# Local values loaded without the overlap of their blocks, the leading rows copied on the chip (strided sparse attention with a bilinear feed-forward layer)

## The chip, the cores and the metric

The kernel runs on one core of one Trainium2 chip. The metric is the device time of one execution in microseconds (us), the median of several runs. The five engines of the core are named as in the profile: PE (TensorE), DVE (VectorE), ACT (ScalarE), POOL (GpSimd) and SP (SyncE). Each works through its own list of instructions in order, and waits for others through semaphores.

## The reference, cut to what matters

Eight batches of eight heads, 576 positions, 64 values per head. Heads 0 to 3 attend to the last 32 positions only ("local"), heads 4 to 7 to positions at multiples of 32 ("strided"). The result, laid out as 4608 tokens of 512 values, goes through `(x @ w_a) * (x @ w_b) @ w_out`.

```python
scores = scale * np.matmul(q, k.transpose(0, 1, 3, 2))
rel = pos[:, None] - pos[None, :]
mask_local = (rel >= 0) & (rel < 32)
mask_strided = (rel >= 0) & (pos[None, :] % 32 == pos[:, None] % 32)
# heads 0..3 take mask_local, heads 4..7 mask_strided; masked scores become -1e9
attn = exp(scores - max) / (sum(exp(scores - max)) + 1e-09)
x = np.matmul(attn, v)            # then to 4608 x 512
out = ((x @ w_a) * (x @ w_b)) @ w_out
```

A local query sees only itself and 31 keys before it. So the kernel cuts the 576 positions of a head into six blocks of 96 queries, and needs for each block 128 keys and values: the 32 rows before the block and its own 96. Successive blocks overlap by 32 rows.

## The kernel before

The local values of a batch stand in a tile `vl_buf[b % 2]`, 128 partitions by 24 blocks (4 heads x 6), each block 64 values, a column of ones for the sums, and space up to 128 columns. Partition 0 to 31 (`PAD = 32`) of a block hold the rows before it, partitions 32 to 127 its own. The transfer reads float32 and writes bfloat16:

```python
def load_vl(b, blocks=(0, HL * 6)):
    t = vl_buf[b % 2]
    f, e = blocks
    if (b, f) == (0, 0):
        f = 1                       # block 0 of batch 0 has no rows before it
    src = bass.AP(tensor=v.tensor, offset=(b * H * S + LW * f - PAD) * D,
                  ap=[[D, 128], [LW * D, e - f], [1, D]])
    nc.gpsimd.dma_start(out=t[:, f:e, 0:D], in_=src)
```

All large loads are issued by POOL (`nc.gpsimd.dma_start`). They use eight semaphores in turn: a load may be issued when the load eight places before it has landed. The end of the list that matters here, with the semaphore number that each takes, is

```text
... wo_sb (2)  wo_sb (3)  wo_sb (4)  wo_sb (5)  vl of batch 1 (6)  [memset vs]
    kl (7) kl (0) kl (1) kl (2)  ql (3) ql (4) ql (5) ql (6)   natk (7) (0) (1) (2)   natq (3) (4) (5) (6)
```

where `kl`, `ql`, `natk`, `natq` are keys and queries of batch 2. The fourth `ql` so waits until the `vl` of batch 1 has landed.

Batch 0 runs in a hand-made order, whose letters are: `T` transposes of q and k, `S` scores (`p` product on PE, `x` exponential on ACT, `m` mask on DVE), `V` the product with the values (`p` on PE, `r` reciprocal and `n` scaling on DVE), `X` the transpose of the result, `F` the first matmuls of the feed-forward layer, `*n` n filler matmuls on PE, `G` the parts of a mask. An ending number is the unit: 0 to 3 are local, 4 to 7 strided. Units 0 and 1 use value blocks 0 to 11, units 2 and 3 blocks 12 to 23.

```python
ORDER = """
    C0 Tk0p *4 Tq0p Tk0e Tq0e *5 Tk1p S1p M Tq1p S1x Tk1e *4 G0 Tq1e S0p S1m G1 C1 Tq2p S0x Tk2p Tq2e S3p Tk2e G2 S3x *3
    V1p S0m *2 S2p V1r S3m V0p S2x Tk3p V0r Tk3e *1 S4p S2m Tq3p S4x V1n Tq3e *4 V0n S5p S5x X0p X0e *2 V2p V2r V3p V2n
    S6p V4p ...
```

Batches 1 to 7 are interleaved with the feed-forward layer of earlier tokens. Batch 1's local values are first used by `V0` in the middle of the first output matmul block; the table says `12.5: "V0 X2"`:

```python
for i in range(G):                  # G = 3 blocks
    for j in range(2):              # 2 heads
        vt = vl_buf[b % 2][:, (2 * c + j) * 6 + 3 * half + i, 0:D + 1]
        ...
        nc.tensor.matmul(of[:, j, i, :w], lhsT=pt, rhs=vt, start=True, stop=True)
```

In the beginning the rows of block 0 of batch 0 come by a transfer of their own (`raw[2]`) and `C1` casts them into place:

```python
nc.sync.dma_start(out=raw[2][PAD:, :D], in_=v[0, 0, 0:LW, :])
...
elif nm == "C1":
    for p in (slice(PAD, 64), slice(64, 128)):
        nc.vector.tensor_copy(vl_buf[0][p, 0, 0:D], raw[2][p, :D])
```

After batch 0, POOL is given this list at its first place (`do(0, ...)`): fill `vl_buf[0]` with ones, weights, `wo_sb`, `load_vl(1)`, fill `vs_buf[0]`, and then `load_qk(2, ...)`.

Of the kernel before, what the change touches and what calls it, by code (L numbers as in the profile page):

```python
# [7 lines left out]
F32 = mybir.dt.float32  # L8
# [6 lines left out]
FIRST_D = 2  # L15
# [6 lines left out]
LW = 96  # L22
PAD = 32
# [7 lines left out]
def kernel(  # L31
# [10 lines left out]
    nc = tc.nc  # L42
    B, H, S, D = q.shape
# [38 lines left out]
    vl_buf = [const.tile([128, HL * 6, VW], BF16, name=f"vl{i}") for i in range(2)]  # L82
# [15 lines left out]
    def consts(i):  # L98
        if i == 0:
            for p in p_buf:  # L100
                nc.vector.memset(p[:, :, W:], 0.0)
        nc.vector.memset(kT_buf[i][0][:, :, 0:PAD], 0.0)
        nc.vector.memset(kT_buf[i][1], 0.0)
        nc.vector.memset(vl_buf[i][:, :, D:D + 1], 1.0)
        nc.vector.memset(vs_buf[i][:, :, :, D:D + 1], 1.0)
        if i == 0:
            nc.vector.memset(vl_buf[0][:PAD, 0, 0:D], 0.0)

    def fill_v(t):
        nc.gpsimd.memset(t[:, :, :, D:] if len(t.shape) == 4 else t[:, :, D:], 1.0)  # L110
# [21 lines left out]
    def mask_local2():  # L132
        nc.vector.tensor_copy(mask_l, msl.unsqueeze(1).to_broadcast([128, 4, LW]))

        nc.vector.memset(mask_l[:PAD, 0], 0)

    def mask_group(part):

        if part == 0:
            cur["mp"] = psum4["tp"].tile([128, S // 2], F32, tag="tp", name="tp")[:NP, :NP]  # L140
            ef = e4.rearrange("p i r -> p (i r)")
            nc.tensor.matmul(cur["mp"], lhsT=ef, rhs=ef, start=True, stop=True)
        elif part == 1:
            nc.vector.tensor_scalar_mul(mss, cur["mp"], -1.0)

            select(mss, ALU.is_ge, 0, [[1, NP]], -1)
        else:

            nc.vector.tensor_scalar(nmask, mss, 1.0, -8e9, op0=ALU.add, op1=ALU.mult)


    def spin(n):
        for _ in range(n):
            nc.tensor.matmul(cur["misc"][:, :224], lhsT=nc.const_aps.tensor(1.0, [128, 128], BF16),  # L154
                             rhs=nc.const_aps.tensor(1.0, [128, 224], BF16), start=True, stop=True)
# [30 lines left out]
    def load_qk(b, strided, heads=range(HL), names="kq"):  # L186
        for nm in names:
            src = {"k": k, "q": q}[nm]
            if b < FIRST_D:
                n, R, h0 = (NP, RS, HL) if strided else (96, RL, 0)  # L190
                w0 = {"k6": 0, "q6": 1536, "k8": 3072, "q8": 5120}[f"{nm}{R}"]
                if b not in shared:
                    shared[b] = nat.tile([128, FG * 5 * SW], BF16, tag="shared", name="shared")
                t = nats[b, nm, strided] = shared[b][:n, w0:w0 + HL * R * D].rearrange("p (h r d) -> p h r d", r=R, d=D)
                hs = slice(heads[0], heads[-1] + 1)
                nc.gpsimd.dma_start(out=t[:, hs], in_=src[b, h0:h0 + HL].rearrange("h (p r) d -> p h r d", r=R)[:, hs])
            elif strided:

                t = nat_s[nm]
                n = 32 if b == FIRST_D else YS  # L200
                for h in heads:
                    nc.gpsimd.dma_start(
                        out=t[32 * h:32 * h + n],
                        in_=bass.AP(tensor=src.tensor, offset=(b * H + HL + h) * S * D,
                                    ap=[[RS * D, n], [YS * RS * D, 3], [1, RS * D]]))
            else:
                if 0 in heads:
                    nats[b, nm, strided] = nat.tile([128, NY, D], BF16, tag=f"{nm}l", name=f"{nm}l")
                t = nats[b, nm, strided]
                for h in heads:  # L210
                    nc.gpsimd.dma_start(out=t[32 * h:32 * h + 32],  # L211
                                        in_=src[b, h].rearrange("(i y) d -> y i d", y=32))
            nats[b, nm, strided] = t

    def load_vl(b, blocks=(0, HL * 6)):

        t = vl_buf[b % 2]
        f, e = blocks
        if (b, f) == (0, 0):
            f = 1  # L220
        src = bass.AP(tensor=v.tensor, offset=(b * H * S + LW * f - PAD) * D,
                      ap=[[D, 128], [LW * D, e - f], [1, D]])
        nc.gpsimd.dma_start(out=t[:, f:e, 0:D], in_=src)

    def load_vs(b, heads=range(HL)):
        if b < FIRST_D:
# [271 lines left out]
    def step_X(b, c):  # L498
# [6 lines left out]
            "Xp": lambda c: X_p(0, c), "Xe": lambda c: X_e(0, c)}  # L505

    ORDER = """
        C0 Tk0p *4 Tq0p Tk0e Tq0e *5 Tk1p S1p M Tq1p S1x Tk1e *4 G0 Tq1e S0p S1m G1 C1 Tq2p S0x Tk2p Tq2e S3p Tk2e G2 S3x *3
        V1p S0m *2 S2p V1r S3m V0p S2x Tk3p V0r Tk3e *1 S4p S2m Tq3p S4x V1n Tq3e *4 V0n S5p S5x X0p X0e *2 V2p V2r V3p V2n
        S6p V4p V3r V3n V4r V4n S6x X1p V5p V5r S7p X1e V5n V6p S7x X2p V6r V7p V6n X2e Z F0a V7r V7n F0b X3p F1a X3e F0c  # L510
        F1b F1c""".split()

# [229 lines left out]
    with tc.manual_schedule(engines={ENG.PE, ENG.SP, ENG.Pool, ENG.DVE, ENG.Activation}):  # L742
# [6 lines left out]
        nc.vector.memset(ident, 1.0)  # L749

        raw = fsb.tile([128, FD, TTOK], BF16, tag="pf", name="raw", bufs=1)
        raw = [raw[:, 3 * i:3 * i + 3].rearrange("p a b -> p (a b)").bitcast(F32) for i in range(3)]
        for x, src in ((raw[0], k), (raw[1], q)):
            nc.sync.dma_start(out=x[:96].rearrange("p (h r d) -> p h r d", h=2, d=D),
                              in_=src[0, 0:2].rearrange("h (p r) d -> p h r d", r=RL))
        nc.sync.dma_start(out=raw[2][PAD:, :D], in_=v[0, 0, 0:LW, :])
        load_qk(0, False, (2, 3))
        load_qk(0, True, (0, 1), "k")
        select(ident, ALU.is_equal, 0, [[1, 128]], -1)
# [12 lines left out]
        for nm in ORDER:  # L772
            if nm[0] == "*":
                spin(int(nm[1:]))
            elif nm == "C0":
                for x, cp, n in ((raw[0], nc.vector.tensor_copy, "k"), (raw[1], nc.scalar.copy, "q")):
                    cp(nats[0, n, False][:, 0:2].rearrange("p h r d -> p (h r d)"), x[:96])
            elif nm == "C1":
                for p in (slice(PAD, 64), slice(64, 128)):
                    nc.vector.tensor_copy(vl_buf[0][p, 0, 0:D], raw[2][p, :D])  # L780
            elif nm == "M":
                mask_local2()
            elif nm[0] == "G":
                mask_group(int(nm[1]))
                if nm == "G1":
                    load_vs(0)
                    for c in range(2):
                        load_w(c)
                    load_w(2)
                    load_qk(1, True)  # L790
                    load_vs(1)
                    load_w(3)
                    load_qk(1, False)
            elif nm == "Z":
                zero_qz(1, nc.scalar, ((0, 0),))
            elif nm[0] == "F":
                f = int(nm[1])
                if nm[2] == "a":
                    if f == 0:
                        ab = pst.tile([128, 2, 512], F32, tag="st", name="ab")  # L800
                        first[f] = [ab[:, 0], ab[:, 1]]
                    else:
                        first[f] = [psum4[x].tile([128, 512], F32, tag=x, name="ab") for x in ("misc", "o")]
                ab_mm(0, f, first[f], {"a": (0, 1), "b": (2,), "c": (3,)}[nm[2]])
            else:
                PART[nm[:-2] + nm[-1]](int(nm[-2]))
# [16 lines left out]
        def do(i, fn, *args):  # L823
            at.setdefault(i, []).append(lambda: fn(*args))
# [8 lines left out]
        for b in range(FIRST_D, B):  # L833
            g0 = 16 * (b - 2)
            if b == FIRST_D:
                do(0, load_qk, b, False)
                do(1, load_qk, b, True)
                do(16, load_vl, b)
                for h in range(HL):
                    do(18 + h, load_vs, b, (h,))  # L840
            else:
                for h in range(HL):
                    do(g0 + h - (0 if b == FIRST_D + 1 else 2), load_qk, b, False, (h,))
                    do(g0 + h + (6 if b == FIRST_D + 1 else 2), load_qk, b, True, (h,))
                    do(g0 + h + 10, load_vs, b, (h,))
                do(g0 + (10 if b == FIRST_D + 1 else 7), load_vl, b)
            gs = {2: (13, 13, 14, 14, 15, 16, 17, 17, 18, 18), 3: (8, 9, 10, 11, 12, 13, 14, 15, 16, 17)}.get(b) or (
                3, 5, 7, 9, 12, 13, 14, 15, 16, 17)
            for (z, nm, part), g in zip(((0, "k", 0), (0, "k", 1), (0, "q", 0), (0, "q", 1), (1, "k", 0), (1, "k", 1),
                                         (1, "k", 2), (1, "q", 0), (1, "q", 1), (1, "q", 2)), gs):  # L850
                do(g0 + g, step_D, b, z, nm, part)
# [62 lines left out]
```

## Time and profile before

| quantity | value |
|---|---|
| time, median of 3 runs | 332.12 us (331.99 to 332.24) |
| span of the profiled execution | 330.0 us |
| PE busy | 322.2 us (98%) |
| DVE, ACT, POOL busy | 263.8, 202.0, 177.5 us |
| packets of the queue that POOL fills (q0) | 87760, 19.58 MB |
| issues of `vl`: 7 of 384.0 KB, one of 192.0 KB, one of 176.0 KB | 7.2, 5.8, 5.3 us to landing |
| granted clock | 1.000 |

The table is read from the top of the page (busy time), its third part (queues) and its sixth (issues). KB there are bytes written, in bfloat16. A busy PE says that matmuls were in flight, not that each was useful: the filler matmuls count as busy too.

### The profile page before, as it was taken

The page shows a single profiled execution, that of the slowest core. Times are in us where ns is not written, and L with a number is a line of the kernel's source. Part 1 is how long each engine was busy: PE and PEld are TensorE (multiplying, and loading weights), DVE is VectorE, ACT ScalarE, POOL GpSimd, SP SyncE. Part 2 cuts the span into 40 slices and gives each one's busy share as a digit, 9 for nine tenths or more (in the row PEclk, how much of TensorE's full clock was granted, in tenths as well). Part 3 has the DMA queues.
Part 4 walks back from the last instruction along what each step waited for, and adds up shares of the span by engine and source line. Part 5 has one row for each costly group of instructions (what it writes and reads, how often), then busy time and mean ns, then how long its engine had stood idle before and what let it go on. Part 6 is the DMA issues. An engine that isn't in the chain of part 4 may idle for free.

```text
span 330.0 us, 7697 instructions
## 1 busy us (share of the span) xinstructions
PE 322.2 (98%) x2819; PEld 206.4 (63%) x2851; DVE 263.8 (80%) x500; ACT 202.0 (61%) x328; POOL 177.5 (54%) x296
## 2 busy tenths in 40 slices
PE   8999999999999999999999999999999999999995
PEld 6754555455555578556999995559555854584474
DVE  5767586779867999999999999999878944657662
ACT  4763946458777865887677766776777543313321
POOL 8945746299967655775578556845302131132021
PEclk9999999999999999999999999999999999999999
DMA  9999999599999698989988978998024022004004
GB/s 156 145 197 189 202 188 190 135 186 108 126 215 125 117 89 74 84 177 154 91 75 153 186 84 74 133 213 92 22 65 125 0 66 65 0 2 127 3 0 127
DMA packets 100661, 37.60 MB, mean 114 GB/s; under 512 B 77456, under 2 KB 97808, under 8 KB 100624
## 3 DMA queue, kind: packets, MB, share of 16 engines
q0 software_dynamic: 87760, 19.58, 65.3%
q1 hardware_dynamic: 12576, 17.34, 18.1%
q8 instruction: 22, 0.36, 0.4%
q10 hardware_dynamic: 288, 0.20, 0.2%
q14 instruction: 15, 0.12, 0.1%
HBM read 39.71 MB, written 9.44 MB: 149 GB/s over the span
## 4 chain that ended last, share of the span: by engine, by line
PE 83%; DMA 12%; POOL 2%; issue 1%; DVE 1%; ACT 0%; POOLq 0%; DVEq 0%
PE mm L546 50%; PE mm L650 17%; DMA vl<-in_v_dram 4%; PE mm L730 4%; PE o L455 4%; PE st L357 4%; DMA shared<-in_k_dram 3%; DMA wa_sb<-in_moe_w_a_dram 3%; PE misc L154 2%; PE mm L678 2%; DMA natk<-in_k_dram 1%; PE end L678 1%; POOL wa_sb L244 0%; POOL wb_sb L244 0%; DVE tk L300 0%
## 5 line engine op out<-in xcount | busy, mean ns | idle before, releaser
L546 PE MATMUL mm<-xT,wa_sb 128*128 128x512 bf16 (+1 forms) x452 | 108.8, 357 | 0.9
L546 PE MATMUL mm<-xT,wb_sb 128*128 128x512 bf16 (+1 forms) x464 | 108.8, 357 | 0.3
L563 ACT COPY a_sb<-mm 128x512 f32<-128x512 f32 x106 | 62.0, 585 | 49.0 <-PE mm L546 46.8
L880 POOL CAST pace<-pf 1x1 f32<-1x1 bf16 x84 | 31.2, 372 | 83.2 <-DVE pf L566 80.7
L546 PEld LDWEIGHTS <-wb_sb 128*128 128x128 bf16 x480 | 46.4, 98 | 44.5 <-issue 0.6
L566 DVE TENSOR_TENSOR pf<-a_sb,mm 128x512 bf16<-128x512 f32 x84 | 56.3, 671 | 17.0 <-PE mm L546 13.7
L546 PEld LDWEIGHTS <-wa_sb 128*128 128x128 bf16 x480 | 42.6, 98 | 31.2
L365 ACT ACTIVATE p<-st 128x576 bf16<-128x576 f32 (+1 forms) x64 | 41.6, 650 | 10.3 <-PE st L357 9.7
L464 ACT ACTIVATE xr<-o 64x576 f32<-64x576 f32 x48 | 31.1, 647 | 25.1 <-PE o L455 24.8
L650 PEld LDWEIGHTS <-ps 128*128 128x128 bf16 x360 | 34.5, 98 | 3.9
L465 ACT ACTIVATE xr<-xr 64x576 f32<-64x576 f32 x48 | 32.8, 683 | 1.5
L469 DVE TENSOR_TENSOR xT<-o,xr 64x288 bf16<-64x288 f32 x48 | 21.5, 448 | 7.7 <-ACT xr L465 7.2
L471 DVE TENSOR_TENSOR xT<-o,xr 64x288 bf16<-64x288 f32 x48 | 21.5, 448 | 6.4 <-ACT xr L465 5.1
L650 PE MATMUL mm<-wf,ps 128*128 128x256 bf16 x216 | 26.4, 273 | 0.0
L375 DVE TENSOR_TENSOR p<-p,mask_l 128x576 int16<-128x576 int16 x32 | 22.3, 697 | 3.4 <-ACT p L365 3.4
L730 PE MATMUL mm<-wo_sb,pf 128*128 128x512 bf16 x93 | 22.7, 379 | 0.6 <-DMA wo_sb<-in_moe_w_out_dram 0.4
L568 DVE TENSOR_TENSOR pf<-a_sb,mm 128x512 bf16<-128x512 f32 x22 | 14.9, 675 | 7.5 <-ACT a_sb L563 5.9
L235 POOL DMA_DIRECT2D vs<-in_v_dram x24 | 19.6, 818 | 2.2 <-PE st L357 2.2
L880 POOL COPY pace<-y_sb 1x1 f32<-1x1 f32 x16 | 2.8, 175 | 31.8 <-ACT y_sb L633 14.6
L211 POOL DMA_DIRECT2D ql<-in_q_dram x24 | 16.0, 668 | 6.2 <-DMA wo_sb<-in_moe_w_out_dram 4.0
L211 POOL DMA_DIRECT2D kl<-in_k_dram x24 | 16.1, 673 | 4.0 <-issue 3.8
L650 PE MATMUL mm<-wf,pf 128*128 128x256 bf16 x144 | 17.6, 273 | 0.0
(151 smaller groups left out, 501.7 us busy)
## 6 DMA issues: line engine op xcount, KB each, us to landing
out_dram<-y_sb SPq DMA_DIRECT2D x12, 512.0 KB, 5.1
vl<-in_v_dram POOLq DMA_DIRECT2D x7, 384.0 KB, 7.2
out_dram<-y_sb SPq DMA_DIRECT2D x10, 256.0 KB, 3.8
kl<-in_k_dram POOLq DMA_DIRECT2D x24, 72.0 KB, 3.4
ql<-in_q_dram POOLq DMA_DIRECT2D x24, 72.0 KB, 3.6
vs<-in_v_dram POOLq DMA_DIRECT2D x24, 72.0 KB, 3.6
wo_sb<-in_moe_w_out_dram POOLq DMA_DIRECT2D x4, 384.0 KB, 11.9
natk<-in_k_dram POOLq DMA_DIRECT2D x20, 72.0 KB, 3.2
```

Of the source, the lines that this page charges most:

```text
L211: nc.gpsimd.dma_start(out=t[32 * h:32 * h + 32], in_=src[b, h].rearrange("(i y) d -> y i d", y=32))
L365: nc.scalar.activation(p[:M, :, :W], st[:M, :, :W], ACT.Exp, scale=scale)
L375: nc.vector.tensor_tensor(pi, pi, mk, op=ALU.bitwise_and)
L464: nc.scalar.activation(r, sums, ACT.Ln)
L465: nc.scalar.activation(r, r, ACT.Exp, scale=-1.0)
L469: nc.vector.tensor_mul(dst[:, W * half:W * (half + 1)], o[:64, j, :W], r[:, j])
L546: nc.tensor.matmul(ps_[:, c0:c0 + n], lhsT=w[:, kk, 128 * f:128 * (f + 1)], rhs=xT[:, kk, x0:x0 + n], start=(kk == first and c0 == 0), sto ...
L563: nc.scalar.copy(a_sb, ab[0])
L566: nc.vector.tensor_mul(pf[:, f, :].rearrange("p (i a s) -> p a i s", i=2, s=16), halves(a_sb), halves(ab[1]))
L650: nc.tensor.matmul(bank[b][:, q], lhsT=lhs(g, q), rhs=rhs(g), start=new and q == 0 and g == 0, stop=g == FG - 1, skip_group_check=True)
L730: nc.tensor.matmul(y, lhsT=pf[:, f, 128 * j:128 * (j + 1)], rhs=wo_sb[:, f], start=(f == 0), stop=(f == FD - 1))
L880: nc.gpsimd.tensor_copy(pace, done)
```

## The change

Local values of batches 0 and 1 are transferred without the 32 leading rows of each block: partitions 32 to 127 only. The leading rows of block n are the last 32 rows of block n - 1, which have landed in partitions 96 to 127, and an on-chip copy brings them to partitions 0 to 31 of the next block. For batch 0 DVE does it in two pieces, `L0` (blocks 1 to 11, placed after `Tk2e`) and `L1` (blocks 12 to 23, placed ahead of `V2p`); for batch 1 POOL does it in one instruction. Block 0 of batch 0 now comes with its load, so `raw[2]` and `C1` go away. Batches 2 to 7 load all 128 partitions as before. The purpose is to move a quarter fewer rows of local values in the part of the program in which most loads are queued.

```diff
-        if i == 0:
-            nc.vector.memset(vl_buf[0][:PAD, 0, 0:D], 0.0)
+        nc.vector.memset(vl_buf[i][:PAD, 0, 0:D], 0.0)
...
-        if (b, f) == (0, 0):
-            f = 1
-        src = bass.AP(tensor=v.tensor, offset=(b * H * S + LW * f - PAD) * D,
-                      ap=[[D, 128], [LW * D, e - f], [1, D]])
-        nc.gpsimd.dma_start(out=t[:, f:e, 0:D], in_=src)
+        p0 = PAD if b < FIRST_D else 0
+        src = bass.AP(tensor=v.tensor, offset=(b * H * S + LW * f - PAD + p0) * D,
+                      ap=[[D, 128 - p0], [LW * D, e - f], [1, D]])
+        nc.gpsimd.dma_start(out=t[p0:, f:e, 0:D], in_=src)
+
+    def lead_vl(eng, b, blocks):
+        t = vl_buf[b % 2]
+        f, e = max(blocks[0], 1), blocks[1]
+        eng(t[:PAD, f:e, 0:D], t[128 - PAD:, f - 1:e - 1, 0:D])
...
-        ... S1m G1 C1 Tq2p S0x Tk2p Tq2e S3p Tk2e G2 S3x *3
-        ... X0p X0e *2 V2p V2r V3p V2n
+        ... S1m G1 Tq2p S0x Tk2p Tq2e S3p Tk2e L0 G2 S3x *3
+        ... X0p X0e *2 L1 V2p V2r V3p V2n
...
-        nc.sync.dma_start(out=raw[2][PAD:, :D], in_=v[0, 0, 0:LW, :])
...
-            elif nm == "C1":
-                for p in (slice(PAD, 64), slice(64, 128)):
-                    nc.vector.tensor_copy(vl_buf[0][p, 0, 0:D], raw[2][p, :D])
+            elif nm[0] == "L":
+                lead_vl(nc.vector.tensor_copy, 0, (12 * int(nm[1]), 12 * int(nm[1]) + 12))
...
             if b == FIRST_D:
                 do(0, load_qk, b, False)
+                do(0, lead_vl, nc.gpsimd.tensor_copy, 1, (0, 24))
                 do(1, load_qk, b, True)
```

The program's order of instructions follows: on POOL the new copy stands behind the fourth `ql` and ahead of the first `natk`. On PE and ACT the lists are the same as before.

More of the change, by code (lines that the diff above doesn't have):

```diff
@@ L507 @@
     ORDER = """
-        C0 Tk0p *4 Tq0p Tk0e Tq0e *5 Tk1p S1p M Tq1p S1x Tk1e *4 G0 Tq1e S0p S1m G1 C1 Tq2p S0x Tk2p Tq2e S3p Tk2e G2 S3x *3
-        V1p S0m *2 S2p V1r S3m V0p S2x Tk3p V0r Tk3e *1 S4p S2m Tq3p S4x V1n Tq3e *4 V0n S5p S5x X0p X0e *2 V2p V2r V3p V2n
+        C0 Tk0p *4 Tq0p Tk0e Tq0e *5 Tk1p S1p M Tq1p S1x Tk1e *4 G0 Tq1e S0p S1m G1 Tq2p S0x Tk2p Tq2e S3p Tk2e L0 G2 S3x *3
+        V1p S0m *2 S2p V1r S3m V0p S2x Tk3p V0r Tk3e *1 S4p S2m Tq3p S4x V1n Tq3e *4 V0n S5p S5x X0p X0e *2 L1 V2p V2r V3p V2n
         S6p V4p V3r V3n V4r V4n S6x X1p V5p V5r S7p X1e V5n V6p S7x X2p V6r V7p V6n X2e Z F0a V7r V7n F0b X3p F1a X3e F0c
@@ L751 @@
         raw = fsb.tile([128, FD, TTOK], BF16, tag="pf", name="raw", bufs=1)
-        raw = [raw[:, 3 * i:3 * i + 3].rearrange("p a b -> p (a b)").bitcast(F32) for i in range(3)]
+        raw = [raw[:, 3 * i:3 * i + 3].rearrange("p a b -> p (a b)").bitcast(F32) for i in range(2)]
         for x, src in ((raw[0], k), (raw[1], q)):
```

## The prediction

> **What bounds the kernel now.** I read the engine table of the page first, then the waits of PE, then the timeline of PE and POOL up to 60 us, where all of the changed work lies, and last the chain that ended last in that stretch.
>
> ```profile
> span 330.0 us, 7697 instructions
> ...
> PE 322.2 (98%) x2819; PEld 206.4 (63%) x2851; DVE 263.8 (80%) x500; ACT 202.0 (61%) x328; POOL 177.5 (54%) x296
> ```
>
> PE is busy for 322.2 of 330.0 us. All idle time of PE together is 7.8 us, and some 4 of these lie behind its last matmul (it starts its last group at 324.69 us and takes 1.49). So what a quicker transfer can give back is what PE spends waiting for transfers. That is in the waits of PE, from 0 to 60 us (engine, line, what it waited for, total, times, longest):
>
> ```profile
> PE misc L154 <- PEq L898: 0.9, 1, 0.9
> PE mm L730 <- DMA wo_sb<-in_moe_w_out_dram: 0.4, 1, 0.4
> PE o L411 <- DVE xr L434: 0.4, 2, 0.2
> ```
>
> One wait for a transfer, 0.4 us, and it is for output weights. Nobody on PE waits for `vl`. This is the ceiling of the direct gain: 0.4 us of 332, far under 2%.
>
> The chain in order of time nevertheless names `vl` (start, length, what):
>
> ```profile
> 25.09 11.34 DMA shared<-in_k_dram
> 36.43 0.92 issue
> 37.35 13.91 DMA vl<-in_v_dram
> 51.26 0.28 issue
> 51.54 0.65 POOL ql L211
> 52.19 2.65 DMA natk<-in_k_dram
> 54.84 0.03 issue
> 54.88 1.43 DVE tk L300 x2
> ```
>
> Here is to be seen that batch 1's `vl` is issued at 37.35 and has landed at 51.26, just before it is needed, and that the fourth `ql` waits for it. The need shows in PE's timeline:
>
> ```profile
> 48.47 0.81 PE L730 MATMUL mm<-wo_sb,pf 128*128 128x512 bf16 x3 [0.43 <-DMA wo_sb<-in_moe_w_out_dram]
> ...
> 51.39 0.34 PE L411 MATMUL o<-vl,p 128*128 128x65 bf16 x6
> ```
>
> The product of batch 1's first local unit (`V0`) starts at 51.39, 0.13 us after the landing. It has no slack to give away.
>
> POOL's timeline shows the queue in front of it:
>
> ```profile
> 48.71 0.66 POOL L211 DMA_DIRECT2D ql<-in_q_dram  x1 [1.25 <-DMA wo_sb<-in_moe_w_out_dram]
> 51.54 0.66 POOL L211 DMA_DIRECT2D ql<-in_q_dram  x1 [2.17 <-DMA vl<-in_v_dram]
> ```
>
> POOL is let go at 48.71 by the last `wo_sb` and at 51.54 by `vl`, so `vl` took 2.83 us of transfer time behind `wo_sb`. It is 128 x 24 = 3072 rows of 64 values: 0.92 ns per row over all transfer engines.
>
> [...] the three `wo_sb` landings release POOL at 44.65, 46.80 and 48.71, and `vl`, issued after them, at 51.54. [...] Rows of `vl` are 256 B read and 128 B written, [...] `vl` needs 2.83 us where a `wo_sb` of the same 384 KB needs some 2.0 (46.80 to 48.71 is 1.91). [...] POOL's subtraction of 512 float32 took 1270 ns and of 256 took 727, so 2.12 ns per element and 0.18 us fixed.
>
> **The change part by part.**
>
> *Rows taken from the queue.* Batch 0: 128 x 11 + 128 x 12 = 2944 rows become 2 x 96 x 12 = 2304, 640 fewer, and the 96 rows of `raw[2]` go as well: 736 x 0.92 ns = 0.68 us, if the queue stays full from there to 50 us. I think it does: from 21 us on POOL is let go by landings every 2 us or so. Batch 1: 3072 becomes 2304, 768 x 0.92 = 0.71 us. So `wo_sb` lands about 0.7 us earlier, `vl` of batch 1 about 0.68 + 0.71 = 1.4 us earlier.
>
> *DVE, batch 0.* Gone: the two casts of `C1` (0.39 us from 9.73). They freed nothing: DVE was then idle for 0.25 us until PE's transposes came at 10.37. Added: one memset of 32 x 32, some 0.03 us of pipelined time, and `L0` with 11 x 64 = 704 elements[...]. `L0` starts when the copy of `kT0s` ends (10.37 + 0.46), so at 10.86 where `nmask` started; the loads that it needs were issued at 4.79 and took 5.3 us, landing about 10.1 before and sooner now. `V1p`, at 10.95 before, then starts at about 11.25: **+0.3 us on PE**. `L1` lies in DVE's 1.21 us of idle time ahead of 15.35 and costs nothing. These 0.3 us stay with PE until a wait on a fixed time takes them up, and that is the 0.43 us for `wo_sb` at 48.47. It vanishes, since `wo_sb` comes 0.7 us earlier: PE reaches `V0` at 51.39 - 0.43 + 0.3 = 51.26.
>
> *POOL, batch 1.* The copy is 23 x 64 = 1472 elements. By the memsets of POOL (1536 elements 1.40 us, 2048 elements 1.82, so 0.83 ns each) it is 1.35 us; by half the two-input slope, 1472 x 1.06 + 0.18 = 1.74. I take the middle, 1.55 us. It stands behind the fourth `ql`, which itself waits for `vl`. So `V0` may start at: 51.54 - 1.4 = 50.14 (`ql` starts) + 0.65 (its issue) + 1.55 (copy) + 0.05 (signal) = **52.39**. Against 51.39 that is **+1.0 us**, and as it is later than 51.26, the early parts don't add to it.
>
> *After that.* PE's next idle times are 0.19 us at 57.03 and less; they hang on ACT and DVE work that itself follows PE, and so move along. I count 0.1 us as taken up. `natk` is issued from about 52.3 instead of 52.19, with its first transpose on DVE not before 60.13: no wait. From 60 us on PE is the bound and passes the delay to the end.
>
> Sum: 332.12 + 1.0 - 0.1 = **333.0 us**.
>
> **The rivals.**
>
> *A. The gain shows and the copy is hidden.* If the queue gains 2.5 us or more instead of 1.4, `V0` finds its values ready, and the total is 0.1 us better or so (0.43 won, 0.3 lost): 332.0. For it: small rows may cost more than 0.92 ns early on, where the moved GB/s is 156 and 145 against 190 later. Against: it would take 1.7 ns per row or more for all 1504 rows.
>
> *B. The copy is slower than I think.* POOL at 2 ns per element would need 3 us: V0 at 53.9, total about 334.5. For it: POOL's two-input rate. Against: one input, and memsets at 0.83. POOL and DVE may also get in each other's way, but DVE is idle from about 50.7 to 51.78.
>
> *C. The early copies bind.* Were `L0` held up by the landing of its load until, say, 11.5, PE would lose 0.6 instead of 0.3. It would be hidden behind the wait for `vl` at 52.39, as up to 1.1 us of early delay is. So C moves the total only together with A, to 332.3.
>
> **Range and chances.** The centre is the wait at `V0`. Its parts: queue gain 0.9 to 2.0, copy 1.3 to 2.0, run to run 0.15. A gives the lower end, a slow copy with a small gain the upper: 332.0 to 334.0. Two per cent are 6.6 us; no part of the change has a size like this in either direction, so "within 2%" has nearly all the chance.
>
> **What the profile after would show.** Right: `wo_sb` no longer in the waits of PE; a wait of PE at `V0` (line of `o<-vl,p`, about 52.4 us) for the POOL copy, 0.8 to 1.3 us; the copy at 1.3 to 1.8 us; `vl` landing near 49.9; `V1p` near 11.25; PE's busy time unchanged but for missing records. Wrong: no wait at `V0` (the queue gained more, or the copy is short), a copy of 0.6 or 3 us, `vl` landing as late as 51 (the queue wasn't full early, or rows aren't what it costs), or a new wait beyond 60 us, which would say that the delayed `natk` or POOL's order matters later than I think.

## The result and the profile after

The changed kernel takes 333.53 us (median of 6 runs, 333.12 to 334.06), the kernel before 332.06 (6 runs, 331.54 to 332.46). The ratio is 1.0045, with a 95% interval of 1.0032 to 1.0058: slower by 0.45%, some 1.5 us. The prediction was 333.0, with 332.0 to 334.0 as its range. Here and below the time of a kernel is the median of all executions, while a ratio and its interval leave out the slow ones (over 1.5% above the fastest).

The head of the page after, span and engine table (busy us, share of the span, number of instructions; PEld is PE's loading of weights):

```profile
span 331.6 us, 7696 instructions
...
PE 321.1 (97%) x2819; PEld 205.7 (62%) x2851; DVE 265.1 (80%) x501; ACT 202.1 (61%) x328; POOL 177.6 (54%) x297
```

The span has grown by 1.6 us while PE's busy time has not, so the loss is waiting. The waits of PE after, up to 80 us (who waited for whom, total, times, longest; L415 is line 415 of the kernel, PEq is PE's own sequencer) name it:

```profile
PE o L415 <- POOL vl L227: 1.4, 1, 1.4
PE misc L153 <- PEq L901: 0.9, 1, 0.9
PE mm L734 <- DMA wo_sb<-in_moe_w_out_dram: 0.5, 1, 0.5
PE tp L274 <- DMA shared<-in_q_dram: 0.5, 1, 0.5
...
PE o L415 <- DVE vl L227: 0.3, 1, 0.3
```

The first line is new: a product with `vl` (L415, `V0` of batch 1) waits for the copy on POOL (L227). The last is new as well: `V1p` of batch 0 waits for `L0`. So is the wait of 0.5 us for queries of batch 0, ahead of `V1p`: PE ran some 0.6 us further ahead at 7 us than in the profile before, and waited there. The wait for the last `wo_sb`, which was to vanish, is still 0.5 us.

The timeline of POOL after, around the copy, to be held against the two lines of before (start, length, engine and line, operation, output and input, count; in brackets the idle time before it and what ended it):

```profile
48.92 0.66 POOL L210 DMA_DIRECT2D ql<-in_q_dram  x1 [1.22 <-DMA wo_sb<-in_moe_w_out_dram]
50.82 0.66 POOL L210 DMA_DIRECT2D ql<-in_q_dram  x1 [1.24 <-DMA vl<-in_v_dram]
51.52 1.40 POOL L227 COPY vl<-vl 32x1472 bf16<-32x1472 bf16 x1
52.88 2.23 POOL L201 DMA_DIRECT2D natk<-in_k_dram  x4
```

The last `wo_sb` lets POOL go at 48.92 (before: 48.71), `vl` 1.90 us later (before: 2.83). Then follow the issue of the fourth `ql` and 1.40 us of copy, to 52.92. And in the timeline of PE after:

```profile
51.36 0.19 PE L415 MATMUL o<-vl,p 128*128 128x65 bf16 x1
52.98 0.31 PE L415 MATMUL o<-vl,p 128*128 128x65 bf16 x5 [1.43 <-POOL vl L227]
```

The first matmul of `V0` uses block 0, whose leading rows are set to zero and not copied, and runs. The other five wait. They begin at 52.98, where before all six began at 51.39: 1.59 us later. The third `V` of batch 1 (58.58 against 57.03) is 1.55 us later, and the last group of matmuls of the program

```profile
326.25 1.49 PE L682 MATMUL mm<-wf,ps 128*128 128x256 bf16 x18
```

(before: 324.69) 1.56. What follows neither adds to the delay nor takes back more than 0.03 us of it.

### The profile page after: what moved, and what is told of

The parts are those of the page before. It is cut to its first block, busy times and chain, and to the rows that moved or that the text cites. A ratio compares the mean times of both kernels' runs of the same rounds, so it can differ in the third digit from the quotient of the medians.

```text
span 331.6 us, 7696 instructions
## 1 busy us (share of the span) xinstructions
PE 321.1 (97%) x2819; PEld 205.7 (62%) x2851; DVE 265.1 (80%) x501; ACT 202.1 (61%) x328; POOL 177.6 (54%) x297
## 4 chain that ended last, share of the span: by engine, by line
PE 75%; DMA 15%; POOL 3%; DVE 3%; issue 2%; ACT 1%; POOLq 0%; SPq 0%; DVEq 0%; ACTq 0%
PE mm L550 45%; PE mm L654 16%; DMA vl<-in_v_dram 4%; PE mm L734 4%; DMA shared<-in_k_dram 4%; PE o L459 4%; PE st L361 3%; DMA wa_sb<-in_moe_w_a_dram 3%; DMA kl<-in_k_dram 2%; PE mm L682 2%; DMA raw<-in_q_dram 1%; DVE tk L304 1%; DMA natk<-in_k_dram 1%; PE end L682 1%; DVE xT L473 1%
```

## The experiments

Three theories stood against each other. **Theory 1**: PE loses what `V0` waits, and that is the landing of `vl`, plus an issue, plus the POOL copy. **Rival 2**: the copies of batch 0 on DVE delay PE for good. **Rival 3**: the rows that are no longer loaded for batch 0 shorten the queue by 0.92 ns each. (In the expectations of runs 5 and 6 "Rival 2" stands for anything else that `V0` may wait for.) The ratios are against runs of the kernel before on the same chip, beside these. Where the quotient of two medians and the ratio differ, the ratio is the one to go by.

| run | time, us | before beside it | ratio, 95% interval | last `wo_sb` / `vl` let POOL go at, us | `V0` runs at, us |
|---|---|---|---|---|---|
| batch 0's part alone | 332.38 | 331.94 | 1.0005 (0.9973 to 1.0036) | 47.93 / 50.52 | 53.12 (no wait) |
| batch 1's part alone | 333.94 | 331.94 | 1.0050 (1.0032 to 1.0068) | 49.12 / 51.25 | 53.41 |
| batch 1's copy on DVE | 332.86 | 331.94 | 1.0017 (0.9992 to 1.0042) | 47.55 / 49.60 | 51.36 |
| the changed kernel again | 333.73 | 331.94 | 1.0039 (1.0016 to 1.0062) | 48.62 / 50.16 | 53.82 |
| copy behind `natq` | 339.43 (1 run) | 331.70 | none | 48.05 / 50.02 | 56.60 |
| copy in two pieces | 333.01 | 331.70 | 1.0034 (1.0008 to 1.0059) | 48.47 / 50.51 | 51.86 |
| batch 0: a third of the rows | 334.29 (1 run) | 331.70 | none | 47.96 / 49.87 | 53.19 |
| the kernel before again | 332.18 (1 run) | 331.70 | none | 48.47 / 51.00 | 50.91 (no wait) |
| DVE copy among the sums | 332.15 | 331.66 | 1.0006 (0.9988 to 1.0025) | 48.17 / 50.08 | 51.39 |
| the same, `L0` earlier | 331.99 | 331.66 | 1.0001 (0.9983 to 1.0019) | 48.77 / 50.79 | 51.20 |
| the kernel before, `Tq1` earlier | 332.00 | 331.79 | 1.0013 (0.9997 to 1.0029) | 48.02 / 50.81 | 51.95 (no wait) |
| 10, and `Tq1` earlier | 331.49 | 331.79 | 0.9997 (0.9981 to 1.0012) | 48.75 / 50.90 | 51.24 |

One single execution stands behind the last two columns of each row. In some of them PE's granted clock fell for a few us before 25 us, as in the first row (0.66 from 10 to 15 and from 20 to 25 us), so `V0` then came late without any wait. In those rows the wait tells more than the place.

**1. Batch 0's part alone**

```diff
-        p0 = PAD if b < FIRST_D else 0
+        p0 = PAD if b == 0 else 0
-                do(0, lead_vl, nc.gpsimd.tensor_copy, 1, (0, 24))
```

> Only batch 0's part of the change: its values are loaded without the overlap and copied by DVE (L0, L1); batch 1 loads all 128 partitions as before, and POOL makes no copy. Theory 1 (the loss is the wait of PE at V0 for batch 1's values, made of landing, the issue of the fourth ql and the POOL copy): no loss here, 332.1, within 0.3 us of the kernel before, V0 at 51.2 to 51.6. Rival 2 (the early copies on DVE delay PE for good): 332.4 or more, V1p some 0.3 us later and the delay still there at 60 us. Rival 3 (the removed rows of batch 0 shorten the queue by 0.7 us, and only the profile of the changed kernel didn't show it): the last wo_sb lands 0.5 us or more earlier than before and its wait vanishes, 331.7.

The ratio is 1.0005, within 0.36% of no change either way, and the profile has no wait at `V0` and none for `wo_sb` (PE came to both late, as its clock had fallen). The whole loss of 0.45% is not here. Whether this part costs or gives 0.3 us can't be told from these times.

**2. Batch 1's part alone** (against the kernel before)

```diff
...
+        p0 = PAD if b == 1 else 0
-        src = bass.AP(tensor=v.tensor, offset=(b * H * S + LW * f - PAD) * D,
-                      ap=[[D, 128], [LW * D, e - f], [1, D]])
-        nc.gpsimd.dma_start(out=t[:, f:e, 0:D], in_=src)
+        src = bass.AP(tensor=v.tensor, offset=(b * H * S + LW * f - PAD + p0) * D,
+                      ap=[[D, 128 - p0], [LW * D, e - f], [1, D]])
+        nc.gpsimd.dma_start(out=t[p0:, f:e, 0:D], in_=src)
...
+                do(0, lead_vl, nc.gpsimd.tensor_copy, 1, (0, 24))
```

> Only batch 1's part: batch 0 loads as before, with its own transfer for block 0 and the two casts; batch 1 loads 96 partitions and POOL copies the leading rows behind the fourth ql. Theory 1: the whole loss is here, 333.3 to 333.7, with a wait of PE at V0 of 1.2 to 1.6 us for the POOL copy. Rival 2: a fifth or more of the loss is missing, 333.2 or less. Rival 3: as batch 0's rows are back in the queue, vl lands later than with the whole change and the loss is larger, 334.0.

The ratio is 1.0050: all of the loss. The waits of PE in this run:

```profile
PE o L417 <- POOL vl L229: 1.7, 1, 1.7
PE mm L736 <- DMA wo_sb<-in_moe_w_out_dram: 0.9, 1, 0.9
```

The wait at `V0` is 1.66 us, a little over the 1.2 to 1.6 of theory 1. The time, 333.94, is over its range too and beside the 334.0 of rival 3; but the interval holds the ratio of the changed kernel again (run 4: 1.0039), so the times don't tell these two apart, and rival 3 is left to runs 7 and 8. Rival 2 is out as the main cause of the loss.

**3. The copy of batch 1 on DVE**

```diff
-                do(0, lead_vl, nc.gpsimd.tensor_copy, 1, (0, 24))
-    ... 12: "Tq1 S1", ...
+    ... 12: "L0 Tq1 S1", ...        # here L0 is DVE's copy for batch 1, behind the sums W0 to W4
...
```

> The whole change, but the copy of batch 1's leading rows is done by DVE between the weight sums and the mask of S1, not by POOL. Then it needs no place behind the fourth ql: it may start when vl has landed (50.5 in the profile of the changed kernel) and DVE is free (50.7 before), takes some 0.55 us, and V0 could start at 51.3 to 51.4. Theory 1: nearly all of the loss is gone, 332.1 to 332.4, the wait at V0 under 0.3 us. Rival 2: 332.4 to 332.7, as the early copies stay. Rival 3: 331.7.

DVE's timeline in this run, behind the last of the weight sums:

```profile
50.76 0.55 DVE L227 COPY vl<-vl 32x1472 bf16<-32x1472 bf16 x1
```

The same 1472 elements take 0.55 us here, 1.40 on POOL, and nothing has to be issued first. `V0` went on at 51.36, as it did before the change, after a wait of 0.58 us: PE had reached it at 50.59, since no wait for `wo_sb` came ahead of it. In the profile the loss is gone, as theory 1 has it. The time, 332.86 at a ratio of 1.0017, is above what was expected and too wide to tell theory 1 from rival 2.

**4. The changed kernel again** (no edit)

> The changed kernel once more, unaltered, to see how much its landings move from one execution to another and to have it timed on the same chip as its parts. All theories: 333.3 to 333.7. Theory 1: the wait at V0 again 1.2 to 1.6 us, V0 at 52.6 to 53.1. Rival 3 would see the last wo_sb land earlier this time, by 48.2.

The time is 0.03 us above the expected range, the wait at `V0` 1.27 us, and the last `wo_sb` came at 48.62, not by 48.2 as rival 3 would have it. `V0` itself is at 53.82, later than expected, for two reasons. PE was late, with a granted clock of 0.72 from 20 to 25 us. And the copy took twice as long. POOL's line, and then DVE's, of this run:

```profile
50.86 2.90 POOL L227 COPY vl<-vl 32x1472 bf16<-32x1472 bf16 x1
```

```profile
50.08 2.42 DVE L174 TENSOR_TENSOR wf<-wo_sb 128x768 bf16<-128x768 bf16 x5
52.99 1.09 DVE L379 TENSOR_TENSOR p<-p,mask_l 128x576 int16<-128x576 int16 x1 [0.50 <-ACT p L369]
```

The copy starts while DVE is among its sums and ends 1.26 us after the last of them (50.08 + 2.42 = 52.50, and 53.76). So of its 1.40 us almost all came after them. The mask behind takes 1.09 us where it takes 0.46 alone. More of this in the last section.

**5. The copy behind `natq`**

```diff
                 do(0, load_qk, b, False)
-                do(0, lead_vl, nc.gpsimd.tensor_copy, 1, (0, 24))
                 do(1, load_qk, b, True)
+                do(1, lead_vl, nc.gpsimd.tensor_copy, 1, (0, 24))
```

> The changed kernel with POOL's copy moved from behind the fourth ql to behind the fourth natq, eight issues later. Theory 1 (V0 waits for the place of the copy in POOL's order): the eight issues take 4.45 us (2.23 + 2.22 in the profile of the changed kernel), so V0 starts at 57.0 to 57.8 and the time is 337 to 338.5. Rival 2 (V0 waits for the landing of vl, or the early part delays PE): 333.3 to 334.

PE's line in this run:

```profile
56.60 0.43 PE L415 MATMUL o<-vl,p 128*128 128x65 bf16 x5 [5.68 <-POOL vl L227]
```

`V0` went on at 56.60, a little before the expected 57.0 to 57.8, as `vl` let POOL go 0.80 us earlier than in the changed kernel (50.02). This shows that the place of the copy in POOL's order sets the wait. The time, 339.43, is above the expected 337 to 338.5: the span grew by 5.7 us over the changed kernel's, `V0` moved by 3.6 only. The rest is seen in PE's windows (stretch, length, PE busy and instructions, granted clock, DMA share, GB/s):

```profile
50.00:55.00 5.00, 0.92 (x6) 0.93 1.65 189
55.00:60.00 5.00, 3.40 (x21) 0.50 0.56 88
60.00:65.00 5.00, 5.00 (x49) 0.89 0.20 67
```

After the idle stretch the granted clock is 0.50, and matmuls take about twice their time until it comes back (six with `wo_sb` 2.75 us, where they take 1.46).

**6. The copy in two pieces**

```diff
-                do(0, lead_vl, nc.gpsimd.tensor_copy, 1, (0, 24))
+                do(0, lead_vl, nc.gpsimd.tensor_copy, 1, (0, 9))
+                do(0, lead_vl, nc.gpsimd.tensor_copy, 1, (9, 24))
```

> The changed kernel with POOL's copy cut in two: first the leading rows of blocks 1 to 8 (512 elements), which are all that V0 uses, then those of blocks 9 to 23. The first piece should take 0.18 + 512 x 0.83 ns = 0.6 us instead of 1.4. Theory 1: V0 starts 0.8 us earlier relative to the fourth ql, and the time is 332.7 to 332.9 where the changed kernel has 333.5 to 333.7. Rival 2: if V0 waits for more than the length of the copy, 333.3 or more. It is also possible that the matmul of V0 is made to wait for both pieces, then 333.6.

PE's timeline in this run:

```profile
50.91 0.19 PE L415 MATMUL o<-vl,p 128*128 128x65 bf16 x1
51.86 0.31 PE L415 MATMUL o<-vl,p 128*128 128x65 bf16 x5 [0.76 <-POOL vl L227]
```

The first piece took 0.60 us, as worked out, and `V0` followed it: 1.35 us behind the moment at which `vl` let POOL go (50.51), where it was 2.16 in the changed kernel (50.82 to 52.98). That is the 0.8 us expected. The time, 333.01 at 1.0034, has not shown it clearly: the interval still holds the changed kernel's ratio, and above the kernel before beside it (331.70) it is 1.3 us. This profile also has another wait of PE, 0.6 us for a transfer of another unit's queries (`qz11s`), which the kernel before had too in its second profile (0.5).

**7. A third of batch 0's rows** (leaves out rows 0 to 63 of every block of batch 0's local values; zeros stand there)

```diff
-        p0 = PAD if b < FIRST_D else 0
+        p0 = 96 if b == 0 else PAD if b == 1 else 0
+        nc.scalar.copy(vl_buf[0][:96, :, 0:D], ...zeros...)
```

> Leaves out work: of batch 0's local values only rows 64 to 95 of each block are loaded (32 partitions instead of 96), and ACT fills the other partitions with zeros at the start, so the result of batch 0's local heads is another. 1536 rows fewer than the changed kernel. Theory 3 (each row in front costs the queue 0.92 ns): everything behind lands 1.4 us sooner than in the other kernels with narrow loads, the third wo_sb at 44.2 to 44.8 us (45.6 to 47.0 there), vl of batch 1 at about 48.3, V0 at 51.3 or so, 332.2. Against it (the queue is held up by POOL's own order or by waits for PE, not by rows): the third wo_sb at 45.6 or later, 333.5.

The third `wo_sb` let POOL go at 45.60, 0.8 us later than the latest that rival 3 expected for 1536 rows fewer, the last at 47.96, `vl` at 49.87 instead of 48.3. One of the other kernels with narrow loads has 45.63 and 47.55. So rows taken from the head of the queue don't bring what lies behind them forward by 0.92 ns each.

**8. The kernel before again** (no edit)

> The kernel before, unaltered, for a second look at its landings. Theory 3: the third wo_sb lands at 46.5 to 47.2 and the wait for the last one is 0.4 to 0.9 us, as in the two profiles with wide loads of batch 0. If it lands at 46.0 or earlier, landings with wide and narrow loads of batch 0 don't differ by more than they move from one execution to the next.

Third `wo_sb` at 46.57, last at 48.47, with a wait of 0.74 us for it: in the expected range. Over all profiles, the last `wo_sb` came at 48.0 to 49.1 in the four kernels that load batch 0 in full (mean 48.58) and at 47.6 to 48.9 in the nine with narrow loads (mean 48.36; run 7 is left out). The ranges overlap, and the difference of 0.2 us is below their spread. The step from there to `vl` doesn't overlap: 2.53 to 2.83 us with 3072 rows of batch 1 (four profiles: the two of the kernel before, runs 1 and 11), 1.54 to 2.15 with 2304 (ten).

**9 and 10. The DVE copy among the sums, and `L0` earlier**

```diff
-    ... 11.5: "V7 W0 W1 W2 W3 W4", ...
+    ... 11.5: "V7 W0 W1 W2 L0 W3 W4", ...                  # 9: L0 as in run 3, without POOL's copy
...
-        ... S1m G1 Tq2p S0x Tk2p Tq2e S3p Tk2e L0 G2 ...
+        ... S1m G1 L0 Tq2p S0x Tk2p Tq2e S3p Tk2e G2 ...   # 10, in addition
```

> A version that may beat both: as with the copy on DVE, but placed between the third and the fourth of the five weight sums, not behind them. In the profile with the copy on DVE, vl had landed at 49.6, the sums ended at 50.7, and V0 waited 0.58 us for the copy although PE had come to it by 50.6. Here the copy may run at 49.7 to 50.3. Theory 1: no wait at V0, and as the wait for wo_sb is gone too, 0.3 to 0.7 us under the kernel before. Where the landings are late DVE waits for vl with two sums behind it, which costs little. Rival 2: the same as before or slower, 332.1 to 332.6, as the early part loses what the queue gains.

> In addition batch 0's first copy L0 stands ahead of the copy of kT0s in DVE's order. In the profiles with narrow loads DVE is idle for about 1.1 us there and V1p waits 0.3 us for L0. Theory: if the first part of vl has landed by 10.1 us, V1p no longer waits, 0.2 to 0.4 us under the version without this. If it lands later than 10.3, the copy of kT0s and the mask work behind it are held up, and it is the same or slower.

With 1.0006 and 1.0001 both are as fast as the kernel before, and the loss of the change is gone, with batch 0's copies still in place. `V0` in the profile of the first:

```profile
51.39 0.35 PE L415 MATMUL o<-vl,p 128*128 128x65 bf16 x6
```

All six matmuls run without a wait. Neither run gives the 0.3 us or more under the kernel before that was hoped for. In the profile of the second, `V1p` runs at 10.54 without a wait for `L0`, and the waits of PE show where the 0.3 us went:

```profile
PE mm L735 <- DMA wo_sb<-in_moe_w_out_dram: 0.9, 1, 0.9
```

PE came earlier to `wo_sb` and waited there for longer.

**11 and 12. The transposes `Tq1` ahead of the wait for `wo_sb`**

```diff
-    11.5: "V7 W0 ...", 12: "Tq1 S1"
+    11.5: "V7 Tq1 W0 ...", 12: "S1"
```

> The kernel before with one thing moved: the transposes Tq1 of batch 1 (0.4 us of PE) stand in the middle of the first output block, ahead of the matmuls that wait for the last wo_sb, instead of behind it. In the two profiles of the kernel before PE waits 0.4 and 0.7 us there. If that wait is what the removed rows could at best give back, filling it with work that is due anyway gives 0.3 to 0.4 us without moving any transfer: 331.3 to 331.4 where the kernel before has 331.7. If V0's values land later than PE then comes to V0, part of it is lost to a new wait there.

> The same move in the version with narrow loads, both copies on DVE, batch 1's among the weight sums, and L0 early. It has the shorter vl transfer as well, so V0 should not wait. Expected 331.1 to 331.4, 0.3 to 0.6 us under the kernel before. If the narrow loads bring nothing, it is equal to the run above.

1.0013 and 0.9997: no gain that these runs can measure. In the profile of the first the wait for `wo_sb` is gone and nothing replaces it at `V0`; but PE's clock had fallen there (0.86 from 15 to 20 us, 0.80 from 20 to 25; 0.993 over the whole execution) and it came late, so this says little of the move. In the second the wait is still 0.5 us, and `V0` waits 0.30 us for DVE's copy. No version here is measurably faster than the kernel before.

## Why the prediction was right, and where its terms were off

- **The ceiling of the gain** (0.4 us, since PE waits for no other transfer): not exceeded. No run with narrow loads is measurably faster.
- **The wait at `V0` behind `vl`, `ql` and the copy**: right, and shown. Batch 1's part alone has the whole loss (run 2). Eight issues later makes the wait 5.7 us (run 5), a shorter first piece brings `V0` 0.8 us nearer to the landing of `vl` (run 6), and with the copy on another engine 0.58 us of the wait is left behind the sums (run 3) and nothing among them (runs 9, 10).
- **The gain of batch 1's rows**, 768 x 0.92 ns = 0.71 us: right, with a little over (2.83 to 1.90 in the first two profiles; the means of all profiles are 2.69 and 1.96).
- **The gain of batch 0's rows**, 736 x 0.92 = 0.68 us "if the queue stays full": this is the term that failed. The changed kernel's profile shows the last `wo_sb` 0.21 us later rather than 0.7 earlier; over all profiles it is 0.2 us earlier, within the scatter, and 1536 more rows taken away (run 7) did not bring it forward by more than that scatter. The cost per row was measured behind the last `wo_sb`, near 50 us, and carried to the first 15 us. That fewer rows in front bring everything behind them forward was the author's assumption, and the runs do not show it.

The traces show from where on the gain is missing. Batch 0's two loads took 5.3 and 5.8 us to landing before, 5.5 and 6.0 in the changed kernel, and still 4.6 and 4.8 with a third of the rows in run 7. And the landing of a `wb_sb` near 23 us, behind all of batch 0's local values, let POOL go at these times before, after and in run 7:

```profile
23.15 0.76 POOL L244 DMA_DIRECT2D wb_sb<-in_moe_w_b_dram  x1 [1.17 <-DMA wb_sb<-in_moe_w_b_dram]
22.80 0.76 POOL L248 DMA_DIRECT2D wb_sb<-in_moe_w_b_dram  x1 [1.17 <-DMA wb_sb<-in_moe_w_b_dram]
22.94 0.76 POOL L248 DMA_DIRECT2D wb_sb<-in_moe_w_b_dram  x1 [1.53 <-DMA wb_sb<-in_moe_w_b_dram]
```

The four profiles with batch 0 in full lie from 22.80 to 23.62 (mean 23.16), the eight with narrow loads in which a landing lets POOL go there from 22.74 to 23.92 (mean 23.15). So nothing was left of the gain by 23 us, and what comes after can't have lost it. Why it is missing was not settled. In run 7 the DMA share from 10 to 15 us falls to 1.06, from 1.25 to 1.44 in the nine other profiles with narrow loads, which would fit transfer engines that run short of work there, POOL issuing one load after another without waiting for a landing; that is argued, not shown. With this term fell the step "the wait for `wo_sb` vanishes": it is 0.5, 0.9 and 0.5 us in the changed kernel and in runs 10 and 12. It is gone in runs 1, 3, 4, 5, 6, 7 and 9, but in runs 1, 4 and 7 with a lower clock ahead of it, which let PE come late, and in run 9 after early waits of 1.2 us for transfers.

- **The copy**, 1.55 us: 1.40 in the undisturbed case. The estimate from POOL's memsets (1.35) was the better of the two: less the fixed 0.18 us, 1.40 is 0.83 ns per element, as theirs. The one from half the two-input slope (1.74) was too high: half of the subtraction's 2.12 ns is 1.06 ns per element, and the copy took 0.83. Rival B's remark that POOL and DVE get in each other's way was set aside because DVE is idle from 50.7 to 51.78. In runs 4 and 7, where `vl` lands while DVE is still at its sums, it does happen (2.90 and 2.56 us instead of 1.40).
- **The sum** for `V0` was 52.39; with the measured terms (50.82 + 0.66 + 0.04 + 1.40 + 0.06) it is 52.98. `vl` let POOL go 0.68 us later than worked out: the last `wo_sb` was 0.89 later, and the step from it to `vl` 0.22 shorter. Less 0.15 of copy, and with 0.06 of small terms, that is the 0.59 us by which `V0` came later than predicted, and it accounts for what 333.0 lacks to 333.53. That the total came so near is in part luck: two errors in the other sense took off 0.37 of the 0.89.
- **The early copies**: `L0` took 0.35 us and `L1` 0.43. The length of `L0` behind the 0.3 us on PE was the author's estimate; the profile before has no such copy. `V1p` came at 11.13 where 11.25 was worked out, after the expected 0.30 us of waiting for `L0`; the place agrees in part by luck, as PE was some 0.6 us ahead at 7 us and then waited 0.49 us for queries. All this is covered up by the later wait, as was said.
- **What comes after**: no new wait beyond 60 us. Of the 0.1 us that was to be taken up, 0.03 to 0.04 was (1.59 to 1.56).

## What to carry to other kernels

A transfer that is trimmed to save rows is only worth what waits for it or for what lies behind it, and here PE waited 0.4 us for one load and not at all for `vl`; the copy that the trimming needs went onto the one path that had no slack, behind an issue on POOL, which took up its instructions in the order of its list (in run 5 `vl` let POOL go at 50.02, and the copy, eight issues later in the list, began at 55.15). Ask of each such copy where it stands in its engine's order, what has to be issued ahead of it, and who takes its result. And a cost per row that was read at one place (0.92 ns, near 50 us) should not be carried to another: 736 rows fewer in the first 15 us brought the last `wo_sb` forward by 0.2 us on average, within the scatter, where 0.68 was counted on.

## What the runs showed of the hardware

In these traces POOL's copy and DVE's operations with two inputs in SBUF, the weight sums and the mask, hardly ran side by side. Beside the sums the copy took 2.90 us (run 4) and 2.56 (run 7), instead of 1.40 in the changed kernel and in runs 2 and 5. It ended 1.26 and 1.27 us after the last of the sums, while the five sums took 2.42 us, as they did before the change. So when the fifth sum of run 4 ended, 1.26 of the copy's 1.40 us were still to come, though it had begun 1.64 us before. In the changed kernel it is the other way about, the copy began first, and in DVE's timeline the mask beside it took

```profile
51.99 1.25 DVE L379 TENSOR_TENSOR p<-p,mask_l 128x576 int16<-128x576 int16 x1 [1.19 <-ACT p L369]
```

instead of 0.46, ending 0.32 us after the copy, which took its 1.40. In run 2 the mask took 1.48 us and ended 0.32 us after the copy as well. By what one holds up the other, the traces do not show.

In run 5, with PE idle for 5.68 us, the granted clock was 0.93 from 50 to 55 us, 0.50 from 55 to 60, 0.89 from 60 to 65 and 1.00 from 65 to 70. This cost some 2 us on top of the waiting, an estimate from the span's 5.7 us and the 3.6 us by which `V0` moved. With the wait of 1.43 us in the changed kernel the clock was 1.00 in all stretches from 45 to 65 us. After how long a wait it falls, these runs do not show.
